# Moving cut steps, key sums and token differences within the hand-written order of a fused attention and feed-forward kernel

## The chip, the cores and the metric

The kernel runs on one core of a Trainium2 chip. The metric is the device time of one execution in microseconds; the time before is the median of three runs. A core has five engines with queues of their own: TensorE (PE, with weight loads PEld), VectorE (DVE), ScalarE (ACT), GpSimd (POOL) and SyncE (SP), which only issues DMAs here. Each engine works through its own list in order, and waits on semaphores for the others.

## The reference

Two blocks follow each other. The first is a linear attention with polynomial sketches, for batch 4, 4 heads, 1088 tokens and head size 32:

```
phi(x) = outer product of (S1 x) and (S2 x), 8 x 8 = 64 features
kv  = sum over tokens of phi(k) v^T        z = sum over tokens of phi(k)
out = (phi(q) kv) / (phi(q) z + 1e-6)
```

Its output, with the heads side by side, is x of 4352 tokens by 128. The second block is a gated feed-forward layer with 1536 hidden columns:

```
y = (silu(x @ w_gate) * (x @ w_val)) @ w_out
```

The weights arrive as 64-bit floats and are turned into 32-bit ones on the chip.

## The kernel before, in words

**Tiling.** Tokens of batch 0 form three blocks (0, 1 and 2, of 384, 320 and 384 tokens); the other batches follow in blocks of up to 480 tokens, the list `line`, from block `HEAD` = 3 on. The hidden dimension is 12 chunks of 128. A *unit* (i, j) is block i with chunk j: the gate and value products, silu, and their product, which goes into a slot of `hbuf` or `late`. A *down* (L1077) multiplies such a hidden tile with `wo` and adds into the block's sum in PSUM. When a block's twelfth down is done, `store` transposes the sum (L1131) and issues its output DMAs on SP.

**Two kinds of unit.** Blocks 0 and 1 use plain matmuls (`unit`, L1025). From block 2 on, each weight and each token block is cut into parts of fewer bits, so that the products run in a faster number format. `cut_weights` makes the parts of three chunks (0 to 2, 3 to 5, and so on, numbered c = 0 to 3) of the gate ("g0" to "g3") or the value weights ("v0" to "v3"), in four steps: the first part w1 on ScalarE (L843), the remainder `low` (L846), the scaled remainder wb on ScalarE (L848), and the difference wd (L851 on VectorE, L855 on GpSimd). "g" pieces and "v0" use VectorE, the other "v" pieces GpSimd. `cut_tokens`, "x" in the lists, makes x1 on ScalarE (L865) and the difference xd on VectorE (L873) in its first step, and x0 (L868) in its second. `start_unit` multiplies the differences ("the first d", L989, two matmuls) and scales the result in place on ScalarE (L992); `finish_unit` adds four matmuls (L1001, L1002), applies silu on ScalarE (L1004) and multiplies on VectorE (L1009). So L1001 can start only when L992 of that unit is done. Three PSUM pairs are in rotation for these units.

**Attention of the later batches** runs between the units. It is a generator, `attentions`, and `parts_of(n)` advances it by n steps. For batch 1 the steps that matter here are: the key features (L377) and their sums over tokens on GpSimd (`feature_sums`, L547); then one step, called here the key sums' group, with the products of keys and values (`key_values`, L388), the next batch's key sketches (L354) and their copies on ScalarE (L590), the sums of the features over tokens by TensorE (`value_sums`, L713), the `fold` on VectorE (L601, L605, L608), and `spread_out` (L723, then six DMAs that move pieces of the tile, then four loads of v, all on SP); then one step with the query sketches (L342), which read what the fold's last line L608 writes, and their copies on ScalarE; then `query_step`, whose first parts on VectorE are the dot product with the sums (L741, L744) and the division (L746 to L748), followed by features (L377) and transposes (L758). `numerators` (L776) reads the transposed features and the spread tile.

**The order.** Nothing here is left to a scheduler: the order of the instructions on each engine is that of the calls in the kernel. The stretch that the change touches is a loop of ND = 19 downs (n = 0 to 18), which runs after blocks 0 and 1 have their units and before the loop over j = 3 to 11 for block 2. In each turn it makes one down, may take a narrowing step of the last output weights, may advance the attention, and makes the cut steps that `steps_at` lists for n. The last-but-one turn begins with `start_unit(2, 3)`. A second `steps_at` lists the cut steps of the loop over j; there, unit (2, j+1) is started, (2, j) finished and one down made in each turn. The third and later entries of "v3" have to be made before chunk 9 is started at j = 8.

Before, the 18th down (n = 13) is the last of block 0, and the key sums' group comes directly behind it; the query sketches come at the end of n = 16, and the first half of `query_step` at n = 17 and 18.

Of the kernel before, what the change touches and what calls it, by code (L numbers as in the profile page):

```python
# [19 lines left out]
def kernel(  # L20
# [962 lines left out]
    def start_unit(i, j):  # L983

        n = blocks[i][1]
        xd = x_parts[i][2][:, 0:n]
        ps = sums_of[i, j] = pair((i, j))[:, :, 0:n]
        for k, w in enumerate((wg, wv)):
            nc.tensor.matmul(  # L989
                ps[:, k], w_parts[id(w), j // 3][2][:, j % 3, :], xd, start=True, stop=True  # L990
            )
        nc.scalar.activation(ps, ps, AF.Copy, scale=-1.0 / WHOLE)  # L992
# [158 lines left out]
    def part(name, i):  # L1151

        next(fills[name, i], None)
# [47 lines left out]
    n = steps[0][1]  # L1201
# [50 lines left out]
    def parts_of(n):  # L1252

        for _ in range(n):
            if ahead[0] not in ("pe", "end"):
                ahead[0] = next(att, "end")
# [60 lines left out]
    def at(*names):  # L1317
        for name in names:
            next(cuts[name], None)

    def next_down():
        if order:
            todo.remove(order[0])
            todo.insert(0, order.pop(0))
        down()

    for z, (i, j) in enumerate(seq):
# [18 lines left out]


    steps_at = {
        0: ("v1", "v2"), 1: ("g1",), 2: ("g2",), 3: ("g1", "v1", "v2"), 4: ("g1",), 5: ("g1", "g2"), 6: ("g2", "v1"),
        7: ("g2", "v2"), 8: ("v3",), 9: ("g3",), 10: ("v0",), 11: ("g0", "x"), 12: ("x",), 14: ("g3",),  # L1350
        15: ("g3",), 18: ("g3",),
    }
    ND = 19
    for n in range(ND):
        if n == ND - 2:
            start_unit(2, 3)
        next_down()
        for p in parts.pop(len(seq) + n, ()):
            part(*p)
        parts_of(n in (0, 1, 2, 3, 4, 13, 16, 17, 18))  # L1360
        at(*steps_at.get(n, ()))


    steps_at = {3: ("v3",), 5: ("v3",), 6: ("v3",), 8: ("v0", "g0"), 9: ("v0", "g0", "g0"), 10: ("v0",)}
    todo.sort(key=lambda x: (order + [x]).index(x))
    x_steps = iter(())
    for j in range(3, NCH):
# [101 lines left out]
```

## Time and profile before

| what | value |
|---|---|
| median of 3 runs | 281.33 us (281.23 to 282.9) |
| profiled execution, whole | 280.94 us |
| its span in the profile | 279.2 us |
| TensorE busy | 269.7 us, 97% |
| VectorE busy | 213.2 us, 76% |
| ScalarE busy | 194.2 us, 70% |
| GpSimd busy | 99.4 us, 36% |
| granted TensorE clock | 0.999 |

The profile is one execution. Its page gives busy times by engine, and the chain of work that ended last, followed back from the end. A timeline gives instructions in order: start, duration, engine, line, operation, output and inputs, shape, how many, and in brackets the idle time before it with what ended that. A list of waits gives the engine and line that waited, what it waited for, the sum in microseconds, how often, and the longest. Each fp32 matmul of a down, of L388, L354, L713 and L342 shows as two records. Ends of matmuls are modelled: they can lie some tenths past the slot in which the next one could start.

The loop of 19 downs and what follows it until the first finished unit of block 2 lie between 55 and 77 us of the span; the loop over j ends near 93 us.

### The profile page before, as it was taken

The numbers are of one execution on the slowest core, as the hardware profiler recorded it, in microseconds if no ns is written. First come the engines' busy times: TensorE is split into PE (matmuls) and PEld (weight loads), VectorE is DVE, ScalarE is ACT, GpSimd is POOL, SyncE is SP. The second block draws the span as 40 slices with busy tenths as digits, with TensorE's granted clock in tenths as the row PEclk, the third lists the DMA queues.
The fourth block names the chain that finished last, engine by engine and source line by source line (L and its number), as shares of the span: only waits on it lengthen the run. The fifth ranks groups of instructions, "written<-read, shape, count | busy, mean of one in ns | idle before, by whom it ended". The sixth has DMA issues, their size and how long they took to land.

```text
span 279.2 us, 5778 instructions
## 1 busy us (share of the span) xinstructions
PE 269.7 (97%) x2193; PEld 200.8 (72%) x2193; DVE 213.2 (76%) x371; ACT 194.2 (70%) x348; POOL 99.4 (36%) x111
## 2 busy tenths in 40 slices
PE   8899999998799999999999999999999999999995
PEld 7545566665686677776667768767887788788994
DVE  3997988997797892787836657867986995978771
ACT  3467666534576587676658898859879788887880
POOL 3314322189020270080014452534435362633420
PEclk9999999999999999999999999999999999999999
DMA  6574195222250023200200010000100200010021
GB/s 196 162 228 113 38 266 166 82 80 82 38 112 2 1 36 112 61 0 0 35 9 9 4 22 13 0 2 6 31 2 0 35 1 0 10 27 1 3 34 28
DMA packets 26140, 14.30 MB, mean 51 GB/s; under 512 B 19841, under 2 KB 24193, under 8 KB 26113
## 3 DMA queue, kind: packets, MB, share of 16 engines
q1 hardware_dynamic: 25456, 13.84, 19.3%
q8 instruction: 17, 0.28, 0.5%
q10 hardware_dynamic: 656, 0.10, 0.2%
q14 instruction: 11, 0.08, 0.1%
HBM read 11.41 MB, written 2.23 MB: 49 GB/s over the span
## 4 chain that ended last, share of the span: by engine, by line
PE 86%; DVE 9%; ACT 1%; DMA 1%; issue 1%; SPq 0%; ACTq 0%; DVEq 0%
PE PS L1077 17%; PE PS L1001 14%; PE PS L989 14%; PE PS L1002 14%; PE PS L1025 10%; PE PS L1072 3%; PE PS L1071 3%; PE PS L1069 3%; PE PS L776 2%; PE PS L342 2%; DMA kld<-in_k_dram 1%; PE PS L354 1%; DVE room L846 1%; PE PS L388 1%; DVE man L277 1%; PE PS L1117 1%
## 5 line engine op out<-in xcount | busy, mean ns | idle before, releaser
L992 ACT ACTIVATE PS<-PS 128x960 f32<-128x960 f32 (+1 forms) x93 | 85.7, 922 | 32.3 <-PE PS L989 30.5
L1009 DVE SCALAR_TENSOR_TENSOR hbuf<-PS,sg 128x480 f32<-128x480 f32 (+1 forms) x93 | 58.5, 629 | 39.6 <-ACT sg L1004 37.5
L1004 ACT ACTIVATE sg<-PS 128x480 f32<-128x480 f32 (+1 forms) x93 | 51.0, 549 | 2.0 <-PE PS L1002 2.0
L1077 PE MATMUL PS<-hbuf,wo 128*128 128x480 f32 (+2 forms) x100 | 41.6, 517 | 0.0
L989 PE MATMUL PS<-xd,graw 128*128 128x480 f32 (+1 forms) x72 | 39.5, 549 | 0.0
L1002 PE MATMUL PS<-x,wb 128*128 128x480 f32 (+1 forms) x93 | 34.5, 371 | 0.0
L989 PE MATMUL PS<-xd,wd 128*128 128x480 f32 (+1 forms) x93 | 34.5, 371 | 0.0
L1001 PE MATMUL PS<-x,w 128*128 128x480 f32 (+1 forms) x93 | 34.4, 370 | 0.0
L1002 PE MATMUL PS<-x,graw 128*128 128x480 f32 (+1 forms) x72 | 26.6, 369 | 0.0
L989 PEld LDWEIGHTS PS<-xd,wd 128*128 128x128 f32 x93 | 17.6, 189 | 10.9 <-issue 6.0
L1077 PEld LDWEIGHTS PS<-hbuf,wo 128*128 128x128 f32 x100 | 18.7, 189 | 5.1 <-issue 0.4
L1025 PE MATMUL PS<-xT,wg 128*128 128x384 f32 (+1 forms) x54 | 21.1, 472 | 0.1
L1025 PE MATMUL PS<-xT,wv 128*128 128x384 f32 (+1 forms) x54 | 20.7, 466 | 0.3 <-DVE wv L286 0.3
L1077 PE MATMUL PS<-hbuf,scaled 128*128 128x480 f32 (+1 forms) x48 | 20.6, 518 | 0.0
L868 POOL TENSOR_TENSOR x<-xT,x 128x480 fp32r<-128x480 f32 (+1 forms) x6 | 7.2, 1195 | 37.6 <-ACT x L865 37.6
L989 PEld LDWEIGHTS PS<-xd,graw 128*128 128x128 f32 x72 | 13.5, 188 | 8.3 <-ACT PS L992 4.1
L1001 PEld LDWEIGHTS PS<-x,w 128*128 128x128 f32 x93 | 17.4, 188 | 2.2
L1002 PEld LDWEIGHTS PS<-x,wb 128*128 128x128 f32 x93 | 17.5, 188 | 2.1
L969 POOL TENSOR_TENSOR hlate<-hbuf,hlate 128x480 fp32r<-128x480 f32 (+1 forms) x12 | 14.3, 1198 | 11.4 <-ACT hlate L968 9.3
L1001 PE MATMUL PS<-x,graw 128*128 128x480 f32 (+1 forms) x48 | 18.1, 378 | 0.0
L1029 ACT ACTIVATE sg<-PS 128x384 f32<-128x384 f32 (+1 forms) x21 | 9.7, 464 | 11.0 <-PE PS L1025 11.0
L1001 PE MATMUL PS<-x,gphq 128*128 128x480 f32 (+1 forms) x45 | 16.9, 376 | 0.0
(201 smaller groups left out, 545.3 us busy)
## 6 DMA issues: line engine op xcount, KB each, us to landing
kld<-in_k_dram SPq DMA_DIRECT2D x4, 544.0 KB, 4.1
vld<-in_v_dram SPq DMA_DIRECT2D x12, 144.0 KB, 4.3
qld<-in_q_dram SPq DMA_DIRECT2D x3, 544.0 KB, 4.9
raw<-in_moe_w_out_dram SPq DMA_DIRECT2D x4, 384.0 KB, 4.5
raw<-in_moe_w_gate_dram SPq DMA_DIRECT2D x3, 384.0 KB, 3.5
raw<-in_moe_w_val_dram SPq DMA_DIRECT2D x3, 384.0 KB, 3.8
out_dram<-o SPq DMA_DIRECT2D x16, 60.0 KB, 2.0
vld<-in_v_dram SPq DMA_DIRECT2D x4, 112.0 KB, 3.0
```

What stands on the lines that cost most here:

```text
L969: add_to(before, y + 2, lambda: nc.gpsimd.tensor_tensor(out=h0, in0=h, in1=whole(h1), op=ALU.subtract))
L989: nc.tensor.matmul(ps[:, k], w_parts[id(w), j // 3][2][:, j % 3, :], xd, start=True, stop=True)
L992: nc.scalar.activation(ps, ps, AF.Copy, scale=-1.0 / WHOLE)
L1001: nc.tensor.matmul(ps[:, k], w1, x1, start=False, stop=False, skip_group_check=True)
L1002: nc.tensor.matmul(ps[:, k], wb, x0, start=False, stop=True, skip_group_check=True)
L1004: nc.scalar.activation(sg, ps[:, 0], AF.Silu, scale=WHOLE)
L1009: nc.vector.scalar_tensor_tensor(out=hj[:, 0:n], in0=ps[:, 1], scalar=WHOLE, in1=sg, op0=ALU.mult, op1=ALU.mult)
L1025: nc.tensor.matmul(o[:, 0:n], w[:, j, :], xT[:, t0 : t0 + n], start=True, stop=True)
L1029: nc.scalar.activation(sg[:, 0:n], g[:, 0:n], AF.Silu)
L1069: nc.tensor.matmul(acc[i][:, 0:n], wd, hd, **sides)
L1071: nc.tensor.matmul(p, w1, h1, start=(j == mine[0]), stop=False)
L1077: nc.tensor.matmul(acc[i][:, 0:n], w, hidden[i, j][:, 0:n], **sides)
```

## The change

The first parts (L843) of g1, g2, v3, g3, v0 and g0 are made at n = 0 and 1, where before g1 and g2 began at n = 1 and 2, v3 and g3 at 8 and 9, v0 and g0 at 10 and 11. The key sums' group moves from n = 13 to n = 15, so behind two more downs. The token cut "x" moves from n = 11 and 12 to n = 16 and 17, behind the fold that the key sums' group issues. The query sketches move from the end of n = 16 to the beginning of n = 18, and `start_unit(2, 3)` comes directly behind them at n = 18 (before: beginning of n = 17). The last three steps of g3 move from n = 14, 15 and 18 to n = 18, and the first two steps of `query_step` behind them. In the loop over j, two steps of v3 move from j = 5 and 6 to 6 and 7.

```diff
     steps_at = {
-        0: ("v1", "v2"), 1: ("g1",), 2: ("g2",), 3: ("g1", "v1", "v2"), 4: ("g1",), 5: ("g1", "g2"), 6: ("g2", "v1"),
-        7: ("g2", "v2"), 8: ("v3",), 9: ("g3",), 10: ("v0",), 11: ("g0", "x"), 12: ("x",), 14: ("g3",),
-        15: ("g3",), 18: ("g3",),
+        0: ("v1", "v2", "g1", "g2"), 1: ("v3", "g3", "v0", "g0"), 3: ("g1", "v1", "v2"), 4: ("g1",),
+        5: ("g1", "g2"), 6: ("g2", "v1"), 7: ("g2", "v2"), 16: ("x",), 17: ("x",), 18: ("g3", "g3", "g3"),
     }
     ND = 19
     for n in range(ND):
-        if n == ND - 2:
+        if n == ND - 1:
+            parts_of(1)
             start_unit(2, 3)
         next_down()
         for p in parts.pop(len(seq) + n, ()):
             part(*p)
-        parts_of(n in (0, 1, 2, 3, 4, 13, 16, 17, 18))
+        parts_of(n in (0, 1, 2, 3, 4, 15))
         at(*steps_at.get(n, ()))
-
-
-    steps_at = {3: ("v3",), 5: ("v3",), 6: ("v3",), 8: ("v0", "g0"), 9: ("v0", "g0", "g0"), 10: ("v0",)}
+    parts_of(2)
+
+
+    steps_at = {3: ("v3",), 6: ("v3",), 7: ("v3",), 8: ("v0", "g0"), 9: ("v0", "g0", "g0"), 10: ("v0",)}
```

On TensorE two downs more stand ahead of L388 then; L354 and L713 follow it, then two downs (three before), L342, the first d, and one down (two before) ahead of the second d.

## The prediction

> **What bounds the kernel now.** I read the page first: busy shares, then the chain of work that ended last.
>
> ```profile
> PE 269.7 (97%) x2193; PEld 200.8 (72%) x2193; DVE 213.2 (76%) x371; ACT 194.2 (70%) x348; POOL 99.4 (36%) x111
> ...
> PE 86%; DVE 9%; ACT 1%; DMA 1%; issue 1%; SPq 0%; ACTq 0%; DVEq 0%
> ```
>
> TensorE is the bound, and the 9% of VectorE on the chain are places where TensorE stood still. No matmul is removed, so only such places can pay. The list of TensorE's waits puts two at its head:
>
> ```profile
> PE PS L342 <- DVE s L608: 2.1, 1, 2.1
> PE PS L713 <- POOL zs L547: 1.1, 1, 1.1
> ```
>
> Both lie in the stage that the change rewrites, and nothing else on the list is over 0.9 us. The timeline of TensorE there (start, duration, group, idle before it):
>
> ```profile
> 63.94 1.21 PE L388 MATMUL PS<-phk,vld 128*32 128x64 f32 x72
> 65.08 1.27 PE L354 MATMUL PS<-s,kT 128*64 128x64 f32 x36
> 67.49 0.32 PE L713 MATMUL PS<-zs,ones 128*32 128x64 f32 x8 [1.14 <-POOL zs L547]
> 67.73 1.88 PE L1077 MATMUL PS<-late,wo 128*128 128x320 f32 x6
> 71.77 1.69 PE L342 MATMUL PS<-s,qT 128*32 128x96 f32 x72 [2.15 <-DVE s L608]
> ```
>
> Batch 1's feature sums arrive late (L713 waits for GpSimd), three downs run, then the query sketches (L342) wait for the fold (L601, L605, L608). Why is the fold late? VectorE and ScalarE in the same stretch:
>
> ```profile
> 66.89 0.96 DVE L851 SCALAR_TENSOR_TENSOR graw<-room,graw 128x384 fp32r<-128x384 f32 x1
> 69.51 0.57 DVE L873 SCALAR_TENSOR_TENSOR xd<-x,xT 128x384 fp32r<-128x384 f32 x1 [1.66 <-ACT x L865]
> 70.00 0.55 DVE L868 TENSOR_TENSOR x<-xT,x 128x384 fp32r<-128x384 f32 x1
> 70.47 0.57 DVE L1131 STREAM_TRANSPOSE o<-PS 128x384 f32<-128x384 f32 x1
> 70.97 0.18 DVE L601 TENSOR_TENSOR fold<-PS,sq 128x64 f32<-128x64 f32 x1
> ...
> 71.49 0.22 DVE L608 TENSOR_TENSOR s<-w,own 128x64 f32<-128x64 f32 x1
> ```
>
> ```profile
> 66.89 0.52 ACT L848 ACTIVATE graw<-room 128x384 fp32r<-128x384 f32 x1 [2.04 <-DVE room L846]
> 67.31 0.51 ACT L843 ACTIVATE w<-wv 128x384 fp32r<-128x384 f32 x1
> ...
> 68.97 0.51 ACT L865 ACTIVATE x<-xT 128x384 fp32r<-128x384 f32 x1
> ```
>
> L713's result was there at 67.8, yet the fold started at 70.97: in VectorE's order it stands behind the token differences L873 and L868, and these wait for x1 (L865), which on ScalarE stands behind one L848 that waited for VectorE until 66.89 and four first parts (L843) queued behind it.
>
> **What the Trainium skill says.** "ScalarE: Activation LUTs", What ACT_TABLE_LOAD costs: an ACTIVATE with immediate operands takes 186 ns + 0.833 ns per column, and neighbours overlap by about 93 ns. At 384 columns that is 506 ns and a step of 413; the trace agrees (0.51, starts 0.41 apart). "SBUF — State Buffer", Who interferes with whom: a VectorE instruction with two SBUF inputs and a GpSimd instruction that reads SBUF exclude each other for a whole instruction, by issue order; with one SBUF input VectorE is free. The trace agrees:
>
> ```profile
> 62.71 1.58 DVE L846 TENSOR_TENSOR room<-wg,gphq 128x384 f32<-128x384 f32 x1
> ...
> 71.80 0.52 DVE L846 TENSOR_TENSOR room<-wg,graw 128x384 f32<-128x384 f32 x1
> ```
>
> The first began 0.10 us after a GpSimd L547 (62.61) and ended 0.34 after that one's end (63.95); the second ran with GpSimd idle. This decides one term below, since the fold now meets:
>
> ```profile
> 67.39 2.27 POOL L855 TENSOR_TENSOR wd<-w,wb 128x384 fp32r<-128x384 f32 x2
> ```
>
> whose second instruction runs from 68.67 to 69.67.
>
> **The change, part by part.**
>
> *First parts of chunks 3 and 0* (four L843) go directly behind the four at 55.78 to 57.02, so to about 57.44 to 59.10 (4 x 0.41). Their buffers are free: the products in the weights' old rooms were made before GpSimd's idle time of 6.78 us that ended at 56.58, and the DMAs had landed. The one at L848 behind them slips from 58.58 to 59.10; the next, at 59.85, doesn't; their reader is GpSimd's L855 at 67.39. Cost 0: ScalarE had 1.04 and 0.75 us idle there, then 3.95. Without that cover it would be 1.6 us on ScalarE.
>
> *Key sums two downs later.* Two downs of 320 columns move ahead of L388; the chain prices two at 1.08 us (four passes). L388 goes from 63.94 to 65.02, L354 ends at about 67.4 instead of 66.35. GpSimd's sums end at 67.44 as before, so L713 stays at 67.49 and its wait of 1.14 shrinks to about 0.1. What L388 and L354 need on VectorE was done by 62.0 and 64.9. Past ScalarE, the key copies (L590) now wait for L354 and come at 67.3 and 67.6, and L865 behind them at about 68.0, 1.0 sooner than before.
>
> *Token differences behind the fold.* VectorE after L851 (end 67.85): L1131 at 67.77 (neighbours overlap by 0.08), L601 0.50 later at 68.27, L605 0.22 later at 68.49, L608 0.30 later at 68.79; these steps are those of the rows above. L1131, L601 and L605 have at most one SBUF input and pass. L608 has two (w, own2), and GpSimd's second L855 started 0.12 us earlier: it is held till 69.67 and ends near 69.85. No row of before shows L608 beside GpSimd, so both ends: not held, 69.0; held, 69.85. I take held, as L846 was with 0.10 us to spare. So L342 starts at 69.9, not 71.77: 1.87 sooner (2.7 if not held). L723 follows at 69.9, L873 and L868 at 70.05 to 71.1 (0.57 and 0.55, GpSimd idle by then); the first d now waits for L873, with all of TensorE queued behind it, but not before 71.6, and x0 is needed at 73.05: both hidden, by 1.0 and 1.9 us.
>
> *Downs beside L342.* Only two stand between L713 and L342 (67.73 to 68.81), so a wait of about 1.1 remains. Behind L342 and the first d (L989) stands one down, not two: the first L1001 comes another 0.54 sooner, if ScalarE follows. L342 ends at 71.59, d at 72.14, L992 runs 72.17 to 72.97, and the one down and second d reach to 72.14 + 0.54 + 0.35 = 73.03. Just covered, where before two downs covered it.
>
> *Last g3 steps.* L846 and L851 run before dot (L741), not round it: 71.1 to 72.0, and dot can't start before the second query copy at about 72.15. Hidden. The L848 of that piece now stands between two L992: it ends at 73.35, the second L992 at 74.1, and its matmuls are due at 74.62. Hidden, 0.5 us to spare.
>
> *Chunk 3's values.* L848 one unit later (unit 6), L855 too. Before, L855 at 80.42 held the L377 beside it to 1.80 us (0.93 and 1.05 for the others); now it falls on a transpose. It is done about 1.6 us before L989 needs it. Worth 0 on TensorE, since VectorE catches up before 85.02 anyway.
>
> *DMAs.* SP's order is unchanged. The four stores behind L1131 start near 68.3 instead of 71.07, the six spread copies and four loads of v follow; the last spread copy was issued at 76.98 and such copies landed in 2.3 to 3.4 us, while their reader L776 began at 86.72: hidden, and both move together.
>
> **Sum.** 1.87 + 0.54 = 2.4 us sooner at the first L1001. By idle time it is the same: 1.14 + 2.15 = 3.3 of waiting before, about 0.1 + 1.1 after, and 0.2 or so because the modelled end of the last down lies past its slot. After that everything is relative: from 75 to 84 TensorE's steps follow each other, the 0.5 us wait at 87.3 (L776 behind L1009) hangs on TensorE's own unit through L1004 and shifts with it, and from 92 to 165 TensorE is busy 73.00 of 73.00 us. Profiled execution: 280.94 (span 279.2 and 1.74 around it) less 2.4 is 278.5. The median shown is 281.33, 0.4 above the profiled one; my forecast for it is 281.33 - 2.4 = 278.9. A difference of 1%, 2.8 us, is about what a measurement of this kernel can tell from none.
>
> **Rivals and chances.**
> - Held fold, as forecast: 278.9. Chance 0.60, spread +-0.4.
> - L608 gets in before GpSimd's second L855: L342 at 69.07, gain 2.7 + 0.54 = 3.2, time 278.1. For it: only 0.12 us decide. Against: L377 was held with 0.02. Chance 0.16.
> - VectorE or ScalarE becomes the bound. Dot moves 74.04 to 72.17, 1.87, and if its chain to the transposes L758 sets L776, the rest is lost: 279.5; if L992 also comes late by half a unit (units of block 2 follow in 1.6 to 1.7), 0.8, about 280.3. For it: VectorE is nearly full from 76 to 88. Against: it idles before L1009 at 85.02, and loses an L851 (0.55) and the held L377 (0.85) from that stretch. Chance 0.17.
> - It doesn't do what it says: another wait of L342 or L713 shows up at the same hour, 281.3. The program's waits of L342 name L608 only. Chance 0.03.
> - Slower: the L848 of g3 blocks ScalarE's queue between two L992, with every later L992 and L1004 behind it and TensorE behind these. It needs L846, due at 71.5; from 73.3 on each microsecond of lateness is one on TensorE, and from 73.3 + 2.4 = 75.7 the kernel is slower than before. A held L846 costs 1.06 (1.58 against 0.52), so four such make it even, and with three more it ends near 284.5. Against: GpSimd is idle then. Chance 0.04.
>
> Range: 277.8 (not held, 0.3 of spread) to 280.3 (the third case), which leaves out some 0.15. Faster by over 1% (below 278.5): the second case and a sixth of the first, 0.26; slower by over 1% 0.03; the rest 0.71.
>
> **What would show it.** L843 eight in a row from 55.78; L713 at 67.5 with nearly no wait; L601 at 68.3; L608 about 1.0 us long (0.22 if not held); L342 at 69.9 with a wait near 1.1; the first L1001 at 73.0; the L776 wait still 0.5. Wrong, if L1001 waits for L992, if dot starts after 72.5, or if a wait after 92 grows.

## The result, and the profile after

The changed kernel takes 278.99 us (median of 8 runs, 278.79 to 280.36), the kernel before 281.6 in the same set (8 runs, 281.23 to 284.21). The ratio is 0.9898, with a 95% interval of 0.9865 to 0.993. The profiled executions are 278.97 us (span 277.3) and 280.94 (span 279.2). The runs of the kernel before, and of e1 below, mostly fall in two groups, near 281.2 us with a granted clock of 0.998 to 1.000 and near 282.6 with 0.993 or 0.994 (one with 0.998), while none of the 50 runs of the other kernels shows the lower clock, so gains are counted from 281.2, the median of the largest set of the kernel before (20 runs, 14 of them near 281.2).

The forecast was 278.9, with 277.8 to 280.3 as its range. The list of TensorE's waits after the change (sum, how often, longest), at its head:

```profile
PE PS L241 <- PEq L1454: 0.9, 1, 0.9
PE PS L342 <- DVE s L608: 0.7, 1, 0.7
PE PS L776 <- DVE hbuf L1009: 0.5, 1, 0.5
PE PS L497 <- ACT kvz L1237: 0.4, 1, 0.4
```

L713's 1.1 us are gone, L342's 2.1 are 0.7, and the rest is as it was. TensorE's timeline after:

```profile
65.25 1.21 PE L388 MATMUL PS<-phk,vld 128*32 128x64 f32 x72
66.39 1.27 PE L354 MATMUL PS<-s,kT 128*64 128x64 f32 x36
67.75 0.32 PE L713 MATMUL PS<-zs,ones 128*32 128x64 f32 x8
68.00 0.81 PE L1077 MATMUL PS<-late,wo 128*128 128x320 f32 x2
68.64 0.70 PE L1077 MATMUL PS<-hbuf,wo 128*128 128x320 f32 x2
70.06 1.69 PE L342 MATMUL PS<-s,qT 128*32 128x96 f32 x72 [0.72 <-DVE s L608]
...
73.19 0.44 PE L1001 MATMUL PS<-x,gphq 128*128 128x384 f32 x1
```

L388 and L354 now fill the time in which L713 stood; only two downs lie between L713 and L342; the first L1001 starts at 73.19 instead of 75.27. (What the cut format is worth shows here too: an L1002 and the L1001 behind it start 0.17 us apart (73.47 and 73.64) for 384 columns, where the chain puts a down of 320 columns in fp32 at 0.54.) VectorE and GpSimd after; the second row of GpSimd is the second of the pair by itself:

```profile
68.03 0.57 DVE L1131 STREAM_TRANSPOSE o<-PS 128x384 f32<-128x384 f32 x1
68.53 0.18 DVE L601 TENSOR_TENSOR fold<-PS,sq 128x64 f32<-128x64 f32 x1
68.75 0.27 DVE L605 TENSOR_REDUCE w<-fold 128x8 f32<-128x64 f32 x1
69.05 0.96 DVE L608 TENSOR_TENSOR s<-w,own 128x64 f32<-128x64 f32 x1
...
70.09 0.51 DVE L873 SCALAR_TENSOR_TENSOR xd<-x,xT 128x384 fp32r<-128x384 f32 x1
```

```profile
67.66 2.27 POOL L855 TENSOR_TENSOR wd<-w,wb 128x384 fp32r<-128x384 f32 x2
...
68.94 0.98 POOL L855 TENSOR_TENSOR wd<-w,wb 128x384 fp32r<-128x384 f32 x1
```

The fold starts at 68.53 instead of 70.97, straight behind the transpose. Its last step, L608, takes 0.96 us instead of 0.22: it starts 0.11 after GpSimd's second L855 and ends at 70.01, just behind that one's end at 69.93.

In the stretch from 64 to 92 us TensorE is busy for 26.70 of 28.00 us, where it was 24.22; from 92 to 165 it is 73.00 of 73.00 in both. The columns are span, length, then busy time and count of TensorE, its weight loads, VectorE, ScalarE and GpSimd, the granted clock, and DMA:

```profile
64.00:92.00 28.00, 26.70 (x340) 19.80 (x338) 23.75 (x42) 16.86 (x32) 7.70 (x8) 1.00 0.26 58
92.00:165.00 73.00, 73.00 (x648) 52.36 (x648) 49.63 (x78) 53.97 (x85) 24.01 (x21) 1.00 0.12 27
```

### The profile page after: what moved, and what is told of

Same layout as the page of the kernel before. It is cut to its first block, busy times and chain, and to the rows that moved or that the text cites. A ratio compares the mean times of both kernels' runs of the same rounds, so it can differ in the third digit from the quotient of the medians.

```text
span 277.3 us, 5778 instructions
## 1 busy us (share of the span) xinstructions
PE 270.1 (97%) x2193; PEld 200.9 (72%) x2193; DVE 213.2 (77%) x371; ACT 193.9 (70%) x348; POOL 99.3 (36%) x111
## 4 chain that ended last, share of the span: by engine, by line
PE 86%; DVE 9%; DMA 2%; ACT 1%; issue 0%; SPq 0%; DVEq 0%
PE PS L1077 17%; PE PS L1001 14%; PE PS L989 14%; PE PS L1002 14%; PE PS L1025 10%; PE PS L1072 3%; PE PS L1069 3%; PE PS L1071 3%; PE PS L776 2%; PE PS L342 2%; DMA kld<-in_k_dram 2%; PE PS L354 1%; DVE room L846 1%; PE PS L388 1%; DVE man L277 1%; PE PS L1117 1%
## 5 line engine op out<-in xcount | busy, mean ns | idle before, releaser
L992 ACT ACTIVATE PS<-PS 128x960 f32<-128x960 f32 (+1 forms) x93 | 85.7, 922 | 31.7 <-PE PS L989 30.7
L1009 DVE SCALAR_TENSOR_TENSOR hbuf<-PS,sg 128x480 f32<-128x480 f32 (+1 forms) x93 | 58.6, 630 | 40.5 <-ACT sg L1004 38.3
L1002 PE MATMUL PS<-x,wb 128*128 128x480 f32 (+1 forms) x93 | 34.5, 371 | 0.0
L1001 PE MATMUL PS<-x,w 128*128 128x480 f32 (+1 forms) x93 | 34.4, 370 | 0.0
L1002 PE MATMUL PS<-x,graw 128*128 128x480 f32 (+1 forms) x72 | 26.6, 369 | 0.0
L868 POOL TENSOR_TENSOR x<-xT,x 128x480 fp32r<-128x480 f32 (+1 forms) x6 | 7.2, 1193 | 37.7 <-ACT x L865 37.7
L1001 PEld LDWEIGHTS PS<-x,w 128*128 128x128 f32 x93 | 17.4, 188 | 2.2
L1002 PEld LDWEIGHTS PS<-x,wb 128*128 128x128 f32 x93 | 17.5, 188 | 2.2
L1001 PE MATMUL PS<-x,graw 128*128 128x480 f32 (+1 forms) x48 | 18.1, 378 | 0.0
L1001 PE MATMUL PS<-x,gphq 128*128 128x480 f32 (+1 forms) x45 | 17.0, 379 | 0.0
```

Source lines behind the costliest of these rows:

```text
L1001: nc.tensor.matmul(ps[:, k], w1, x1, start=False, stop=False, skip_group_check=True)
L1002: nc.tensor.matmul(ps[:, k], wb, x0, start=False, stop=True, skip_group_check=True)
L1009: nc.vector.scalar_tensor_tensor(out=hj[:, 0:n], in0=ps[:, 1], scalar=WHOLE, in1=sg, op0=ALU.mult, op1=ALU.mult)
```

## The experiments

Theory: the gain comes from VectorE's order. The fold stood behind two token differences, and stands in front of them now; the rest is arrangement of downs, and L608's hold beside GpSimd (the expectations call the rule behind it the theory of the port) costs what is left. Rivals: the four first parts that left ScalarE's queue are the cause (x1 comes sooner without them); or the key sums' move is, as it ends L713's wait. The query sketches, the first d and the last steps of g3 were not moved back one by one; what is said of them is read from the order and the hours.

One table carries most of the readings. Profiled executions differ by up to 0.3 us before this stage, so the hours are counted from a mark that no edit touches, the start of GpSimd's last L547 (66.52 before, 66.76 after). The gain is 281.2 less the median. The ratios given with the runs are each against the kernel before in the run's own set, whose median was 281.2 for e1, e2, e4 and the repeat, and 282.52 for e3, e6, e7 and e8.

| kernel | end of L608 | L342 | first L1001 | L1001 sooner | median, us | gain |
|---|---|---|---|---|---|---|
| before | 5.19 | 5.25 | 8.75 | | 281.2 | |
| e1, first parts alone | 5.05 | 5.10 | 8.60 | 0.15 | 281.19 | 0.0 |
| e2, x behind the fold alone | 3.24 | 3.29 | 7.22 | 1.53 | 279.71 | 1.5 |
| e7, both | 3.23 | 3.28 | 6.91 | 1.84 | 279.35 | 1.85 |
| e3, changed kernel, key sums at 13 | 3.24 | 3.58 | 6.70 | 2.05 | 279.22 | 2.0 |
| changed kernel again | 3.23 | 3.29 | 6.41 | 2.34 | 278.88 | 2.3 |
| e4, changed kernel, L608 not held | 2.51 | 2.57 | 5.69 | 3.06 | 278.26 | 2.9 |

**The changed kernel again**, as the measure for those that follow.

> The changed kernel once more, beside the parts of it. 2.0 to 2.8 us below the kernel before (ratio 0.990 to 0.993). L608 again about 1.0 us long, TensorE's wait at L342 about 0.7 us.

278.88 us (6 runs, 278.71 to 279.1), ratio 0.9898 (0.9872 to 0.9925). L608 takes 0.95 us and the wait at L342 is 0.72, as expected.

**e1: only the first parts sooner, on the kernel before.**

```diff
-        0: ("v1", "v2"), 1: ("g1",), 2: ("g2",), 3: ("g1", "v1", "v2"), 4: ("g1",), 5: ("g1", "g2"), 6: ("g2", "v1"),
-        7: ("g2", "v2"), 8: ("v3",), 9: ("g3",), 10: ("v0",), 11: ("g0", "x"), 12: ("x",), 14: ("g3",),
+        0: ("v1", "v2", "g1", "g2"), 1: ("v3", "g3", "v0", "g0"), 3: ("g1", "v1", "v2"), 4: ("g1",), 5: ("g1", "g2"), 6: ("g2", "v1"),
+        7: ("g2", "v2"), 11: ("x",), 12: ("x",), 14: ("g3",),
```

> The first parts alone are moved; all else is as before. x1 (L865) comes at 67.3 to 67.8 and no longer holds VectorE. Theory of the port (L873 and L868 have two SBUF inputs and meet GpSimd's two L855): L873 is held to 68.7, GpSimd's second L855 then goes ahead of L868, and L608 ends near 71.6, so that L342 starts at 71.6 where it started at 71.77: gain 0 to 0.3 us. Rival, the order of the queue alone: L873, L868, L1131 and the fold follow each other from 67.85 in their own 0.5 us each, and L342 starts at 70.1: gain 1.6 us.

281.19 us (14 runs, 280.86 to 283.13), ratio 1.0001 (0.9979 to 1.0023). ScalarE does make x1 sooner, at 67.64 instead of 68.97, and the differences start at once. VectorE in this kernel:

```profile
68.17 1.27 DVE L873 SCALAR_TENSOR_TENSOR xd<-x,xT 128x384 fp32r<-128x384 f32 x1
69.37 1.34 DVE L868 TENSOR_TENSOR x<-xT,x 128x384 fp32r<-128x384 f32 x1
70.63 0.57 DVE L1131 STREAM_TRANSPOSE o<-PS 128x384 f32<-128x384 f32 x1
71.13 0.18 DVE L601 TENSOR_TENSOR fold<-PS,sq 128x64 f32<-128x64 f32 x1
...
71.65 0.23 DVE L608 TENSOR_TENSOR s<-w,own 128x64 f32<-128x64 f32 x1
```

and GpSimd beside it:

```profile
67.72 2.58 POOL L855 TENSOR_TENSOR wd<-w,wb 128x384 fp32r<-128x384 f32 x2
...
68.98 1.31 POOL L855 TENSOR_TENSOR wd<-w,wb 128x384 fp32r<-128x384 f32 x1
```

L873 and L868 took 0.57 and 0.55 when GpSimd was idle; here, beside two L855, they take 1.27 and 1.34, and the L855 themselves 2.58 instead of 2.27. The fold starts at 71.13, on the mark only 0.15 sooner than before. This is what the Trainium skill says in "SBUF — State Buffer", Who interferes with whom: a VectorE instruction with two SBUF inputs and a GpSimd instruction that reads SBUF contend. (L1131, which reads PSUM, keeps its 0.57 in the changed kernel, where it runs beside L855.) So the first rival falls: in front of the fold, the two token differences cost nearly as much held beside GpSimd as they did waiting for x1.

**e2: only the token cut behind the fold, on the kernel before.**

```diff
-        7: ("g2", "v2"), 8: ("v3",), 9: ("g3",), 10: ("v0",), 11: ("g0", "x"), 12: ("x",), 14: ("g3",),
+        7: ("g2", "v2"), 8: ("v3",), 9: ("g3",), 10: ("v0",), 11: ("g0",), 13: ("x", "x"), 14: ("g3",),
```

> The token differences alone go behind the fold (both steps at n = 13, behind the key sums' group); the first parts stay where they were, and the key sums too. Theory that the fold's place in VectorE's order is the cause: L608 is held to 69.76, L342 starts at 69.8 with a wait near 0.45 us, L713 still waits 1.1. ScalarE is late behind the first parts (key copies to 69.65, x1 to 70.05, the query copies to 73.05), so L1001 waits some 0.4 us for L992: gain 1.0 to 1.6 us. Rival, that the first parts on ScalarE are the cause: gain under 0.5 us.

279.71 us (7 runs, 279.6 to 280.0), ratio 0.9932 (0.9906 to 0.9957). One line of the schedule brings 1.5 of the 2.3 us. TensorE in this kernel:

```profile
67.73 0.32 PE L713 MATMUL PS<-zs,ones 128*32 128x64 f32 x8 [1.15 <-POOL zs L547]
67.98 1.88 PE L1077 MATMUL PS<-late,wo 128*128 128x320 f32 x6
70.05 1.69 PE L342 MATMUL PS<-s,qT 128*32 128x96 f32 x72 [0.19 <-DVE s L608]
...
73.98 0.44 PE L1001 MATMUL PS<-x,gphq 128*128 128x384 f32 x1 [0.26 <-ACT PS L992]
```

L342 gains 1.96 us on the mark, with three downs still ahead of it and L713's wait whole. Of this 0.43 is lost again until the first L1001, which waits 0.26 for ScalarE's L992. The gain is in the forecast range; the wait at L342 was put near 0.45 and shows as 0.19, since the trace counts it from the modelled end of the last down (67.98 + 1.88 = 69.86).

**e7: both, e1's and e2's edits together.**

> First parts sooner and token differences behind the fold, both; the key sums, the query sketches, the first d, g3 and v3 are as before. Theory: L342 starts as early as in the changed kernel, with 21 and not 22 downs before it, so that one down more (0.54 us) stands behind it ahead of the first L1001: 1.6 to 1.9 us below the kernel before, 0.4 to 0.6 above the changed one. Rival, that these two edits carry all of the gain: equal to the changed kernel.

279.35 us (6 runs, 279.07 to 279.48), ratio 0.9903 (0.9876 to 0.9929). The first parts, worth nothing alone, are worth about 0.3 here: L342 is where e2 has it, but L992 starts 0.30 sooner on the mark (72.74, in e2 73.11), and the first L1001 with it.

```profile
69.97 1.69 PE L342 MATMUL PS<-s,qT 128*32 128x96 f32 x72 [0.18 <-DVE s L608]
...
72.05 1.24 PE L1077 MATMUL PS<-hbuf,wo 128*128 128x320 f32 x4
...
73.60 0.45 PE L1001 MATMUL PS<-x,gphq 128*128 128x384 f32 x1
```

```profile
71.50 0.53 ACT L848 ACTIVATE graw<-room 128x384 fp32r<-128x384 f32 x1 [2.90 <-DVE room L846]
71.93 0.92 ACT L590 COPY qab<-PS 128x480 f32<-128x480 f32 x2
72.74 1.74 ACT L992 ACTIVATE PS<-PS 128x768 f32<-128x768 f32 x2
```

The rest of the change (key sums, query sketches, first d, last steps of g3) is worth the 0.47 between this and the changed kernel (0.4 to 0.6 expected). ScalarE's rows show how: L1001 starts at 73.60, just behind the first L992 (0.80 long, so to 73.54), and this stands behind the query copies, which stand behind g3's L848. In the changed kernel that L848 comes after L992, the copies start at 71.16, and L992 ends 0.47 sooner on the mark.

**e3: the changed kernel with the key sums back at n = 13.**

```diff
-        parts_of(n in (0, 1, 2, 3, 4, 15))
+        parts_of(n in (0, 1, 2, 3, 4, 13))
```

> The changed kernel with the key sums' group back at n = 13, so that its two downs stand behind L713 again (four there, none ahead of L388). Theory: L713 is set by GpSimd's sums (67.44 in the profile of before) and L342 by the fold, so the two downs only move from one wait into the other: the wait of 1.15 us at L713 is back, the one at L342 falls from 0.7 to under 0.1, and the time is that of the changed kernel within 0.2 us. Rival, that the filled wait at L713 is a gain of its own: 0.9 to 1.1 us above the changed kernel.

279.22 us (6 runs, 279.0 to 279.62), ratio 0.9901 (0.9871 to 0.9931): 0.34 over the changed kernel, more than the theory's 0.2 and a third of what the rival asked.

```profile
67.73 0.32 PE L713 MATMUL PS<-zs,ones 128*32 128x64 f32 x8 [1.15 <-POOL zs L547]
67.98 1.88 PE L1077 MATMUL PS<-late,wo 128*128 128x320 f32 x6
69.70 0.70 PE L1077 MATMUL PS<-hbuf,wo 128*128 128x320 f32 x2
70.33 1.69 PE L342 MATMUL PS<-s,qT 128*32 128x96 f32 x72
```

L713's wait of 1.15 is back, but L342's is gone: the two downs only stand in the one hole or in the other, as the end of the second is set by the fold. They don't fit quite. From 67.98 four downs at 0.54 take 2.16, to 70.14 and, as the trace has it, to 70.33, where the fold was ready at 69.99. That overrun, 0.29 on the mark against the changed kernel again, is nearly the whole worth of the key sums' move.

**e4: L608 not held.** In the changed kernel the last difference of v2, the second of GpSimd's two L855, is made on VectorE (as L851, like those of the g chunks) at the end of n = 18.

```diff
-    def cut_weights(w, c, low, engine):
+    def cut_weights(w, c, low, engine, last=None):
...
-        if engine is nc.vector:
+        if (last or engine) is nc.vector:
...
-        cuts["v%d" % c] = cut_weights(wv, c, lows["v%d" % c], nc.gpsimd if c else nc.vector)
+        cuts["v%d" % c] = cut_weights(wv, c, lows["v%d" % c], nc.gpsimd if c else nc.vector, nc.vector if c == 2 else None)
...
-        5: ("g1", "g2"), 6: ("g2", "v1"), 7: ("g2", "v2"), 16: ("x",), 17: ("x",), 18: ("g3", "g3", "g3"),
+        5: ("g1", "g2"), 6: ("g2", "v1"), 7: ("g2",), 16: ("x",), 17: ("x",), 18: ("g3", "g3", "g3", "v2"),
```

> The changed kernel, with the last step of v2 made on VectorE behind the last g3 step, so that GpSimd has one L855 and not two when the fold comes; L608 starts 0.1 us after the end of that one. Theory of the port: L608 takes 0.22 us, L342 starts 0.74 us sooner and TensorE's wait there falls from 0.7 to about 0.1: 0.6 to 0.8 us below the changed kernel. Rival, that L608 is long for another reason (or that dot, 0.3 us later behind one more L851, becomes the bound): 0 to 0.3 us.

278.26 us (6 runs, 277.93 to 279.72), ratio 0.989 (0.9857 to 0.9923). VectorE and GpSimd:

```profile
69.01 0.22 DVE L608 TENSOR_TENSOR s<-w,own 128x64 f32<-128x64 f32 x1
```

```profile
67.61 1.31 POOL L855 TENSOR_TENSOR wd<-w,wb 128x384 fp32r<-128x384 f32 x1
```

With GpSimd idle from 68.92, L608 takes 0.22 us, L342 and the first L1001 come 0.72 sooner on the mark, and L342 no longer waits. The median falls by 0.62; its six runs spread over 1.8 us, so the trace is the firmer number. So the hold is real and costs what L608's length says, 0.96 less 0.22. (The one L855 left takes 1.31 us, as the first of the pair does in the kernel before too: it starts beside an L851 that reads two SBUF inputs.)

**e6: chunk 3's values at the old units, on the changed kernel.**

```diff
-    steps_at = {3: ("v3",), 6: ("v3",), 7: ("v3",), 8: ("v0", "g0"), 9: ("v0", "g0", "g0"), 10: ("v0",)}
+    steps_at = {3: ("v3",), 5: ("v3",), 6: ("v3",), 8: ("v0", "g0"), 9: ("v0", "g0", "g0"), 10: ("v0",)}
```

> The changed kernel with the last two steps of v3 back at j = 5 and 6. Theory of the port: GpSimd's L855 falls on the second L377 again and holds it to about 1.8 us (0.95 in the changed kernel), and VectorE takes that up in its gaps of 0.26, 0.24 and 0.26 us before the three L1009 that follow: 0 to 0.15 us above the changed kernel. Rival, that VectorE sets the pace there: 0.5 to 0.85 us above it.

278.90 us (6 runs, 278.71 to 280.6), ratio 0.9898 (0.9866 to 0.9929): no difference. VectorE in this kernel, and then in the changed kernel:

```profile
78.23 1.80 DVE L377 TENSOR_TENSOR phq<-qab 128x768 f32<-128x768 f32 x1
79.96 0.55 DVE L1009 SCALAR_TENSOR_TENSOR hbuf<-PS,sg 128x384 f32<-128x384 f32 x1
```

```profile
78.47 0.95 DVE L377 TENSOR_TENSOR phq<-qab 128x768 f32<-128x768 f32 x1
79.68 0.56 DVE L1009 SCALAR_TENSOR_TENSOR hbuf<-PS,sg 128x384 f32<-128x384 f32 x1 [0.26 <-ACT sg L1004]
```

A held L377 costs VectorE 0.85 us, and nothing comes of it: in the changed kernel VectorE has gaps ahead of L1009 that take it up, and two L1009 further on it is level again (82.82 in e6, 83.05 in the changed kernel, 16.28 and 16.29 on the mark).

**e8: e4, and L1009 ahead of chunk 0's two remainders.** After all this the 0.5 us wait of L776 for L1009 still stood. In e4 L1009 (84.55) stands on VectorE behind two L846 (83.65 and 84.08).

```diff
-    steps_at = {3: ("v3",), 6: ("v3",), 7: ("v3",), 8: ("v0", "g0"), 9: ("v0", "g0", "g0"), 10: ("v0",)}
+    steps_at = {3: ("v3",), 6: ("v3",), 7: ("v3",), 9: ("v0", "g0", "v0", "g0", "g0"), 10: ("v0",)}
```

> The kernel with the last step of v2 on VectorE, and with the remainders (L846) of v0 and g0 made at j = 9 and not 8, so that they stand behind the L1009 that TensorE waits for at L776 and not ahead of it. Theory: that wait of 0.5 us goes, and the time falls by 0.3 to 0.5 us against the kernel without this edit (278.26). Rival: the wait moves on, to the copies L793 or the next L992: 0 to 0.2 us.

277.57 us (5 runs, 277.32 to 277.64), ratio 0.9839 (0.981 to 0.9868), the best of all. TensorE in e4, then in e8:

```profile
83.98 0.68 PE L776 MATMUL PS<-phT,spread 32*32 32x288 f32 x6
85.16 1.51 PE L776 MATMUL PS<-phT,spread 32*32 32x256 f32 x58 [0.50 <-DVE hbuf L1009]
```

```profile
84.02 2.11 PE L776 MATMUL PS<-phT,spread 32*32 32x288 f32 x64
```

L776 is done at 86.13 instead of 86.67, 0.54 sooner. The medians differ by 0.69, more than the 0.3 to 0.5 expected; e4's runs spread over 1.8 us, and the spans of the two profiled executions differ by 0.6 (276.5 and 275.9), so no second cause is claimed. The edits of e4 and e8 together take 1.3 us off the changed kernel, one by asking what its wait's producer runs beside, one by asking what stands ahead of it on its engine.

## Why the prediction was right

By its own steps, in its order.

- *What bounds the kernel*: TensorE, rightly, but one line of the page is misread. VectorE's 9% of the chain is about 25 us, and TensorE stood still for 279.2 less 269.7, 9.5 us in all; most of that 9% ran beside a busy TensorE. The sum doesn't rest on it, but on the list of waits.
- *First parts, cost 0*: right. Eight L843 run in a row from 56.02, 0.41 apart; the L848 behind them starts at 59.33 and the next at 60.10. But the prediction gave them no worth either. Alone they have none (e1), beside the moved token cut about 0.3, through an earlier L992 (e7 against e2).
- *Key sums two downs later*: the hours are right (L388 at 65.25, L354's end at 67.66, L713 at 67.75 with no wait; on the mark 0.02 later than before). The second count, by idle time, adds the vanished 1.14 us in; that is sound as a total, but it doesn't say what the move is worth: undone, it costs 0.34 (e3), since L713's 1.15 comes back but L342's 0.72 goes. The main sum, 1.87 + 0.54, didn't lean on it.
- *Token differences behind the fold, L342 1.87 sooner*: 5.25 to 3.30 on the mark, 1.95. The fold started at 68.53, and 0.24 of the 0.26 past the forecast hour are the whole trace's.
- *L608 held, 1.0 long*: 0.96. This was the choice between two ends, and the rule of the Trainium skill ("SBUF — State Buffer", Who interferes with whom) decided it rightly with 0.12 us to spare. By the trace it was 0.11: the second L855 began at 68.94, L608 at 69.05. In all six traces where it meets the pair (the changed kernel twice, e2, e3, e6, e7) L608 starts 0.11 or 0.12 behind and takes 0.95 to 0.97, so it wasn't the luck of one execution. One figure under this step is off: the GpSimd sum beside the held L846 ended at 63.88 (62.61 + 1.27), not at 63.95, where the next one starts. What the rival, L608 in first, would have been worth is seen in e4, which removes the cause: priced at 0.8 us at L342, it is 0.72 there, and 0.62 in the time.
- *A wait of about 1.1 at L342*: 0.72 is shown. By slots it is 70.06 less 68.00 + 1.08 = 0.98; the trace counts from the last down's modelled end, 69.34. That term was worked out by slots and should have been given by ends.
- *One down fewer ahead of the second d, 0.54; just covered*: 0.37. From L342 to the first L1001 it was 3.50 us and is 3.13. The prediction's own hours say so too: from 69.9 to 73.03 is 3.13, so they give 2.24 us at the first L1001 where its sum says 2.4. "Just covered" failed by about 0.17 us: the first L1001, at 73.19, starts behind L992 (end 73.14). An L1001 that waits for L992 was one of the three signs of being wrong. The list of waits doesn't show it, as the modelled end of the second d (72.85 + 0.34) hides it, but in all six traces with one down there (the changed kernel twice, e3, e4, e6, e8) L1001 starts 0.04 or 0.05 us after that end. So it is ScalarE that sets this hour, not the down. ScalarE in the changed kernel:

```profile
71.16 1.14 ACT L590 COPY qab<-PS 128x480 f32<-128x480 f32 x2 [2.49 <-PE PS L342]
72.34 0.80 ACT L992 ACTIVATE PS<-PS 128x768 f32<-128x768 f32 x1
73.05 0.52 ACT L848 ACTIVATE graw<-room 128x384 fp32r<-128x384 f32 x1
73.46 0.80 ACT L992 ACTIVATE PS<-PS 128x768 f32<-128x768 f32 x1
```

- *Last g3 steps*: hidden, rightly, but worth more than the nothing it was given. The L848 between two L992 cost TensorE nothing that its list of waits shows, and where it stood before, ahead of the query copies, it made L992 late (e7), so that, by these hours, one down fewer would have gained little there; the slower rival needed it to come after 73.3, and it came at 73.05, because L846 had run at 71.00 unheld. Dot started at 72.33 against 72.15, just under the 72.5 set as the limit.
- *Chunk 3's values, worth 0*: right, by e6.
- *The rest is relative*: right. L776's wait is still 0.5, and the stretch from 92 to 165 is as full as before.

The sum was 2.4: 1.87 + 0.54. At the first L1001 it is 2.32 on the mark, 1.95 + 0.37, two small errors of opposite sign. One unit on (L1001 at 76.85 before, 74.88 after) it is 2.21, as the first L1001 behind the gap takes 0.44 us and not 0.34. Less the 0.24 by which the trace after is already later when the stage starts, that is the 1.97 between the two profiled executions. By medians it is 2.3 from 281.2 and 2.6 from the 281.6 of the same set. So the mechanism was right, and the size within some 0.2 us; that 278.9 meets 278.99 so closely is in part luck, as it starts from yet another median, 281.33.

## What to carry to other kernels

Look for what stands ahead of a wait's producer in its own engine's order before looking at what the producer computes: one line of a schedule brought 1.5 of 2.3 us here (e2), and another some 0.6 more (e8). Before crediting an earlier input, ask what its reader will then run beside; a VectorE step with two SBUF inputs that starts beside GpSimd can lose all of it. And of two waits in a row of which the second ends at an hour set elsewhere, filling the first mostly moves the idle time (e3).

## What was not expected of the hardware

Both engines pay for a meeting, and they take turns, one instruction each. In e1 VectorE's L851 ends at 68.17, GpSimd's first L855 at about 69.0 (the second starts at 68.98), L873 at 69.44, the second L855 at 70.29 and L868 at 70.71. VectorE's two steps took 1.27 and 1.34 us for 0.57 and 0.55, the second L855 1.31 for 1.00. And in the two cases at hand the loss went with how much of the other's instruction was left, not with the step's own size: L608, 64 columns, took 0.96 us for 0.22 and ended 0.08 after GpSimd; L377, 768 columns, took 1.80 for 0.95 in e6 and ended 0.81 after (80.03, L855 at 79.22). Each lost 0.74 to 0.85 us to an L855 of 1.0 that had started just before it.
